# Attention scores on a TensorE-bound kernel: the high-key, low-query term as two products of depth 64 on the two halves of the array's rows

## The chip, the core and the metric

One NeuronCore of one Trainium2 chip runs the whole program. The metric is the time of one execution on the device in microseconds. The kernel before takes 2532.4 us, the median of three runs (2531.88 to 2532.54).

## The reference

Three stages follow each other; everything is float32.

```python
# attention without softmax: u, v [4, 3072, 256], z [4, 3072, 64]
scores = (1 / S) * matmul(z, z.T)
x = u * matmul(maximum(scores, 0) ** 2, v)
# a gated feed-forward (d_ff 1024) on x mixed with the row before it
k = maximum(xk @ w_k, 0);  x = sigmoid(xr @ w_r) * (k * k @ w_v)
# a product of two projections (d_ff 1536)
out = ((x @ w_a) * (x @ w_b)) @ w_out
```

Keys and queries of the scores are the same tensor z, of depth 64; so the matrix of scores is symmetric.

## The kernel before, in words

TensorE multiplies in a rounded form of float32 (`F32R`). To keep the precision of float32, an operand is split into a rounded high part and the rest, the low part, and a product is made of several: high x high, low x high, high x low (`mm3`, L101 to L104).

The attention (`attention`, one call for each of 4 batches x 6 blocks of 512 queries) goes over key blocks of 512 in pairs of 128-key tiles. A pair is one unit of work. Since the scores are symmetric, only blocks with key block >= query block are computed (`scored`); the others are read back from DRAM, where the transposed block was stored (`mirrored`). 42 pairs of a batch are scored, 30 mirrored; over four batches 168 and 120.

A key block lies in `kt` (128 partitions x 512): one half of the partitions holds the 64 dimensions of the high part, the other half those of the low part, and which half is which alternates with the number of the block (`n = s % 2` in `z_prep`). A query block lies in `q` (128 x 2 x 512): `q[:, 0]` is the high part, once in each half of the partitions, `q[:, 1]` the low part, also twice. One matmul of depth 128 with `q[:, 0]` so gives (key high + key low) x query high, one with `q[:, 1]` gives (key high + key low) x query low. For each of the two tiles these two follow each other into one half of a two-bank tile `sc` (L485, L486). ScalarE takes `sc` to `p` (Relu, then Square, L498 and L499), VectorE transposes `p` to store it (L505), ScalarE or VectorE rounds it to `hi` and VectorE makes `lo` (L544 to L547). Then come twelve matmuls of depth 128 into `acc` (two tiles x two halves of v x three).

The order of the work is written out by hand. `units` holds, for each unit, a function that emits the scores and one that emits the twelve value products; the latter follow `AHEAD` = 3 pairs later, so that the scores of a unit stand in front of the value products of an earlier one on TensorE. Work on the side (loads, splits, decoding of weights for later stages) is hung on units by number with `at(i, fn)` and `in_turn(i, ...)`; instructions are emitted in that order, and each engine runs its own in order. Pools of buffers set when a tile may be written again.

z comes in through `z_load` (two blocks of 512 at once, in squares of 32 x 32, by SP's queue), into a tile `zn` of the pool `zp` (one buffer); VectorE transposes the squares from there into `zt` (pool `ztp`, two buffers); `high` and `low` make `kt` of it. The first batch's blocks 2 to 5 come through `zs`.

Of the kernel before, what the change touches and what calls it, by code (L numbers as in the profile page):

```python
# [8 lines left out]
F32 = mybir.dt.float32  # L9
F32R = mybir.dt.float32r  # L10
U32 = mybir.dt.uint32
I32 = mybir.dt.int32
AF = mybir.ActivationFunctionType
ALU = mybir.AluOpType

P = 128
QB = 512
SQ = 32
# [10 lines left out]
def tile_kernel(  # L29
# [29 lines left out]
    nc = tc.nc  # L59
    B, S, D = u.shape  # L60
    DK = z.shape[2]
# [17 lines left out]
    late = {}  # L79
    early = ctx.enter_context(ExitStack())  # L80
    psw = early.enter_context(tc.tile_pool(name="psw", bufs=2, space=bass.MemoryType.PSUM))
    zp = early.enter_context(tc.tile_pool(name="zp", bufs=1))
    ztp = early.enter_context(tc.tile_pool(name="ztp", bufs=2))
    ktp = early.enter_context(tc.tile_pool(name="ktp", bufs=NQB))
    cw = early.enter_context(tc.tile_pool(name="cw", bufs=10))
    turned = early.enter_context(tc.tile_pool(name="turned", bufs=2))
    pmp = early.enter_context(tc.tile_pool(name="pmp", bufs=3))
# [29 lines left out]
    def in_turn(i, *fns):  # L117

        for n, fn in enumerate(fns):
            at(i + n, fn)  # L120
# [236 lines left out]
        at(i, load)  # L357


    zn_t, zt_t, kt_t, v_t, q_t, x_t = {}, {}, {}, {}, {}, {}  # L360

    def z_load(b, s, t=None, queues=()):


        if t is None:
            t = zp.tile([P, QB // SQ, SQ], F32, tag="zn", name="zn")
        for n in range(2):
            src = z[b, (s + n) * QB : (s + n + 1) * QB, :].rearrange("(b i) (a j) -> a i b j", i=SQ, j=SQ)
            for a in range(DK // SQ):
                c = n * DK + a * SQ  # L370
                (queues[a] if queues else nc.sync).dma_start(t[c : c + SQ], src[a])
        zn_t[b, s] = t

    def z_prep(b, s):

        n = s % 2
        h, l = (slice(m * DK, (m + 1) * DK) for m in (n, 1 - n))

        def turn():
            t = zt_t[b, s] = zt_t[b, s + 1] = ztp.tile([P, QB], F32, tag="zt", name="zt")  # L380
            raw = zn_t.pop((b, s)).rearrange("p b j -> p (b j)")
            if b or s:
                nc.vector.transpose(t, raw)
            else:
                nc.vector.transpose(t[:DK], raw[:DK])
                return lambda: nc.vector.transpose(t[DK:], raw[DK:])

        def high():
            kt_t[b, s] = ktp.tile([P, QB], F32R, tag="kt", name="kt")
            if b or s < 2:  # L390
                nc.scalar.activation(kt_t[b, s][h], zt_t[b, s][h], AF.Copy)
            else:
                nc.vector.tensor_copy(kt_t[b, s][h], zt_t[b, s][h])

        def low():
            nc.vector.tensor_tensor(kt_t[b, s][l], zt_t[b, s][h], kt_t[b, s][h].bitcast(F32), op=ALU.subtract)

        return turn, high, low

    def turned_order(t):  # L400

# [6 lines left out]
    def q_prep(b, s):  # L408


        def half(h):
            kt = kt_t[b, s].bitcast(F32)
            if h == 0:
                q_t[b, s] = g_tile([P, 2, QB], F32R, "q")
            q = q_t[b, s]
            m = h ^ s % 2
            k = turned_order(kt[m * DK : (m + 1) * DK])
            nc.vector.tensor_copy(by_order(q[0:DK, h, :]), k)  # L418
            nc.scalar.activation(by_order(q[DK : 2 * DK, h, :]), k, AF.Copy)

        return lambda: half(0), lambda: half(1)
# [48 lines left out]
    def attention(i):  # L470
# [4 lines left out]
        def scored(kb, pr, here):  # L475

            st = {}
            turn = kb > qb

            def a():  # L480
                sc = psw.tile([P, 2, QB], F32, tag="sc", name="sc")
                for t in range(2):
                    c = (2 * pr + t) * P
                    k = kt_t[b, kb][:, c : c + P]
                    nc.tensor.matmul(sc[:, t, :], k, q_t[b, qb][:, 0, :], start=True, stop=False)  # L485
                    nc.tensor.matmul(sc[:, t, :], k, q_t[b, qb][:, 1, :], start=False, stop=True)  # L486
                p = cw.tile([P, 2, QB], F32, tag="cw", name="p")
                if here == 0:
                    hi = cw.tile([P, 2, QB], F32R, tag="cw", name="hi")
                    lo = cw.tile([P, 2, QB], F32R, tag="cw", name="lo")  # L490
                    for t in range(2):
                        nc.scalar.activation(p[:, t, :], sc[:, t, :], AF.Relu, scale=1.0 / S)
                        nc.scalar.activation(p[:, t, :], p[:, t, :], AF.Square)
                        nc.vector.tensor_copy(hi[:, t, :], p[:, t, :])
                        nc.vector.tensor_tensor(lo[:, t, :], p[:, t, :], hi[:, t, :].bitcast(F32), op=ALU.subtract)
                    st["p"] = hi, lo
                    return
                nc.scalar.activation(p, sc, AF.Relu, scale=1.0 / S)  # L498
                nc.scalar.activation(p, p, AF.Square)  # L499
                if turn:  # L500
                    if pr == 0:
                        x_t["turned"] = turned.tile([P, QB // SQ, TPB, SQ], F32, tag="t", name="pt")
                    pt = x_t["turned"]
                    for t in range(2):
                        nc.vector.transpose(  # L505
                            pt[:, :, 2 * pr + t, :], p[:, t, :].rearrange("p (c i) -> p c i", i=SQ)
                        )
                    if pr:
                        d = p_kept[b, kb, qb] = dram.tile(
                            [P, QB // SQ, TPB, SQ], F32, tag=f"p{b}.{kb}.{qb}", name="pkept"  # L510
                        )
                        at(here + 3, lambda: nc.gpsimd.dma_start(d, pt))
                st["p"] = halves(p, turn and (i or pr))


            return st, a
# [97 lines left out]
        if qb == 0:  # L614
            for s in range(0 if b else 1, NQB):
                need = base + s * TPB
                turn, high, low = z_prep(b, s)
                if b:
                    w = base - 16 + (s - NQB + 2) * NKT - 8 * (s < NQB - 1)
                    if s % 2 == 0:  # L620
                        at(w - 6, lambda s=s: z_load(b, s))
                        at(w + 4, turn)
                    in_turn(w + 6, high, low)
                    at(base - 22 + 4 * s, lambda s=s: v_load(b, s))
                    in_turn(base - 16 + 4 * s, *v_prep(b, s))
                    continue
                if s > 1:
                    if s % 2 == 0:
                        at(need - 13, turn)
                    in_turn(max(need - 11, 0), high, low)  # L630
                else:
                    early_z.append((high, low))
                in_turn(need - 1, *v_prep(b, s))
        if i:
            in_turn(base - 7, *q_prep(b, qb))
# [981 lines left out]

    with tc.manual_schedule():
        z_load(0, 0, None, (nc.sync, nc.scalar))
        zs = g_tile([P, 2, QB // SQ, SQ], F32, "zs")  # L1620
        z_load(0, 2, zs[:, 0])
        v_load(0, 0)
        z_load(0, 4, zs[:, 1])
        for n in range(1, NQB):
            v_load(0, n)
        for c, m in enumerate((mu_k, mu_r)):
            nc.sync.dma_start(mu[:, c, :], m.rearrange("(d p) -> p d", p=P))
        turn, high, low = z_prep(0, 0)
        turn_next = turn()
        for fn in (high, low, *q_prep(0, 0), turn_next, *early_z[0]):  # L1630
            fn()
        for n, fn in enumerate(v_prep(0, 0)):
            at(n // 2, fn)
        last = max(len(units), max(sides) + 1)
        for i in range(last):
            if i == n1:
                while pending:
                    pending.popleft()()
                early.close()
                late["ps"] = ctx.enter_context(  # L1640
                    tc.tile_pool(name="psp", bufs=4, space=bass.MemoryType.PSUM, reuse_waits="tile")
                )
                late["p"] = ctx.enter_context(tc.tile_pool(name="late", bufs=24, reuse_waits="tile"))
            for fn in sides.get(i, ()):
                fn()
            if i < len(units):
                a, b, ahead = units[i]
                if a is not None:
                    a()
                if b is not None:  # L1650
                    pending.append(b)
            else:
                ahead = 0
            while len(pending) > ahead:
                pending.popleft()()
# [27 lines left out]
```

## Time and profile before

| | |
|---|---|
| median of three runs | 2532.4 us |
| the profiled execution | 2532.29 us |
| its span, first to last instruction | 2530.5 us |
| TensorE matmul, busy | 2515.5 us, 99% |
| VectorE, busy | 2192.0 us, 87% |
| ScalarE, busy | 1833.7 us, 72% |
| granted TensorE clock | 1.00 of full speed in every slice |

Engines: PE is TensorE's matmul, PEld its loading of weights, DVE VectorE, ACT ScalarE, POOL GpSimd, SP the queue that issues most loads. L485 is line 485 of the kernel. A matmul's record is longer than the distance to the next one, since matmuls are pipelined; the step from start to start is what a matmul costs. The attention takes the span up to about 945 us; the other two stages follow.

### The profile page before, as it was taken

How to read it: one execution, taken by the hardware profiler on the slowest of the kernel's cores; microseconds unless marked ns; L12 is line 12 of the kernel's file. 1: busy time of each engine (PE TensorE's matmuls, PEld its weight loads, DVE VectorE, ACT ScalarE, POOL GpSimd, SP SyncE). 2: the span in 40 equal slices, each digit the busy share in tenths (PEclk: the TensorE clock that was granted, in tenths of full speed). 3: DMA queues.
4: the chain of work that ended last, by engine and by line, in shares of the span. 5: the costliest groups of instructions: out<-in, count | busy, mean ns of one | idle time of the engine just before them, and what ended most of it. 6: DMA issues, size and time to landing. Idle time of an engine off the chain costs nothing.

```text
span 2530.5 us, 32287 instructions
## 1 busy us (share of the span) xinstructions
PE 2515.5 (99%) x11062; PEld 2072.0 (82%) x11062; DVE 2192.0 (87%) x3081; ACT 1833.7 (72%) x2571; POOL 334.9 (13%) x347
## 2 busy tenths in 40 slices
PE   8999999999999999999999999999999999999999
PEld 6888888888888888888888888888888888888887
DVE  9998999899988987888888878888888888888887
ACT  7866977787687758878878766666666766666665
POOL 0110111010000100000000012222222222222211
PEclk9999999999999999999999999999999999999999
DMA  8789789887986894212122156665766675666664
GB/s 216 220 234 239 237 238 232 232 259 219 254 238 200 227 265 155 67 59 92 51 83 67 59 180 219 210 224 184 260 197 231 196 244 196 233 214 220 213 195 138
DMA packets 326629, 486.85 MB, mean 192 GB/s; under 512 B 188800, under 2 KB 202112, under 8 KB 318784
## 3 DMA queue, kind: packets, MB, share of 16 engines
q1 hardware_dynamic: 302880, 372.71, 51.5%
q0 software_dynamic: 21984, 111.42, 11.4%
q8 instruction: 87, 1.43, 0.2%
q10 hardware_dynamic: 1600, 0.66, 0.1%
q14 instruction: 78, 0.64, 0.1%
HBM read 348.13 MB, written 136.58 MB: 192 GB/s over the span
## 4 chain that ended last, share of the span: by engine, by line
PE 98%; DVE 1%; ACT 0%; DMA 0%; issue 0%; DVEq 0%
PE px L1152 15%; PE acc L103 10%; PE acc L104 10%; PE acc L102 10%; PE py L1152 8%; PE vacc L720 6%; PE px L784 5%; PE oacc L1183 4%; PE oacc L1182 4%; PE oacc L1181 4%; PE vacc L744 4%; PE pw L1152 4%; PE sc L486 3%; PE sc L485 3%; PE py L784 3%; PE pw L784 1%
## 5 line engine op out<-in xcount | busy, mean ns | idle before, releaser
L103 PE MATMUL acc<-lo,vhi 128*128 128x512 f32 x1152 | 449.1, 390 | 1.7 <-DVE lo L547 1.4
L102 PE MATMUL acc<-hi,vhi 128*128 128x512 f32 x1152 | 448.4, 389 | 1.1 <-DVE hi L546 1.1
L104 PE MATMUL acc<-hi,vlo 128*128 128x512 f32 x1152 | 448.2, 389 | 0.0
L1152 PE MATMUL px<-t,sw 128*128 128x512 f32 x1296 | 364.3, 389 | 0.0
L1152 PEld LDWEIGHTS px<-t,sw 128*128 128x128 f32 x1296 | 243.0, 188 | 51.2 <-DVE cc L1337 0.6
L103 PEld LDWEIGHTS acc<-lo,vhi 128*128 128x128 f32 x1152 | 216.2, 188 | 49.3 <-DVE lo L547 3.9
L102 PEld LDWEIGHTS acc<-hi,vhi 128*128 128x128 f32 x1152 | 216.2, 188 | 46.8 <-DVE hi L546 1.5
L104 PEld LDWEIGHTS acc<-hi,vlo 128*128 128x128 f32 x1152 | 216.2, 188 | 44.6
L1237 ACT ACTIVATE pw<-px 128x512 f32<-128x512 f32 x144 | 83.8, 582 | 201.3 <-PE px L1152 201.3
L498 ACT ACTIVATE p<-sc 128x1024 f32<-128x1024 f32 x167 | 170.1, 1018 | 69.2 <-PE sc L486 68.1
L1349 POOL TENSOR_TENSOR cc<-cc 128x512 f32<-128x512 f32 x72 | 93.2, 1294 | 873.8 <-DVE b L1203 663.6
L1249 DVE TENSOR_TENSOR u<-py,u 128x512 f32<-128x512 f32 x144 | 99.6, 691 | 124.5 <-PE py L1152 124.5
L547 DVE TENSOR_TENSOR lo<-p,hi 128x1024 fp32r<-128x1024 f32 x167 | 199.9, 1197 | 4.2
L499 ACT ACTIVATE p<-p 128x1024 f32<-128x1024 f32 x167 | 177.3, 1062 | 5.3
L505 DVE STREAM_TRANSPOSE pt<-p 128x512 f32<-128x512 f32 x240 | 155.7, 687 | 25.4 <-ACT p L499 24.9
L1292 ACT ACTIVATE c<-pw 128x512 f32<-128x512 f32 x144 | 86.3, 600 | 110.3 <-PE pw L1152 80.6
L547 DVE TENSOR_TENSOR lo<-pm,hi 128x1024 fp32r<-128x1024 f32 x120 | 145.9, 1217 | 19.7 <-ACT hi L544 19.4
L1347 POOL TENSOR_TENSOR cc<-cc 128x512 f32<-128x512 f32 x71 | 91.7, 1291 | 439.5 <-DVE bl L1203 219.0
L720 PE MATMUL vacc<-kh,w 128*128 128x512 f32 x416 | 143.4, 389 | 0.0
L485 PE MATMUL sc<-q,kt 128*128 128x512 f32 x336 | 132.0, 393 | 6.5 <-DVE q L418 6.4
L544 ACT ACTIVATE hi<-pm 128x1024 fp32r<-128x1024 f32 x120 | 124.8, 1049 | 16.3 <-DMA pm<-pkept 14.2
L486 PE MATMUL sc<-q,kt 128*128 128x512 f32 x336 | 131.7, 392 | 0.0
(251 smaller groups left out, 6111.5 us busy)
## 6 DMA issues: line engine op xcount, KB each, us to landing
sw<-kept SPq DMA_DIRECT2D x252, 512.0 KB, 5.4
pkept<-pt POOLq DMA_DIRECT2D x60, 1024.0 KB, 6.1
pm<-pkept SPq DMA_DIRECT2D x240, 256.0 KB, 6.6
ow<-kept SPq DMA_DIRECT2D x120, 512.0 KB, 6.8
kept<-w POOLq DMA_DIRECT2D x42, 512.0 KB, 5.0
vst<-in_v SPq DMA_DIRECT2D x24, 512.0 KB, 6.8
ust<-in_u SPq DMA_DIRECT2D x192, 64.0 KB, 4.4
xkept<-xr POOLq DMA_DIRECT2D x24, 512.0 KB, 6.4
```

Source lines behind the costliest of these rows:

```text
L102: nc.tensor.matmul(ps, wh, ah, start=first, stop=False)
L103: nc.tensor.matmul(ps, wh, al, start=False, stop=False)
L104: nc.tensor.matmul(ps, wl, ah, start=False, stop=last)
L485: nc.tensor.matmul(sc[:, t, :], k, q_t[b, qb][:, 0, :], start=True, stop=False)
L486: nc.tensor.matmul(sc[:, t, :], k, q_t[b, qb][:, 1, :], start=False, stop=True)
L498: nc.scalar.activation(p, sc, AF.Relu, scale=1.0 / S)
L499: nc.scalar.activation(p, p, AF.Square)
L505: nc.vector.transpose(pt[:, :, 2 * pr + t, :], p[:, t, :].rearrange("p (c i) -> p c i", i=SQ))
L547: nc.vector.tensor_tensor(l, p, h.bitcast(F32), op=ALU.subtract)
L720: nc.tensor.matmul(acc[n, d], x[:, c], y, start=first and m == 0, stop=last and m == 2, skip_group_check=True)
L784: nc.tensor.matmul(bank, w[x][:, c], t[:, y, :], start=first and m == 0, stop=end and m == 2, skip_group_check=True)
L1152: nc.tensor.matmul(bank, w, t[:, y, :], start=first and m == 0, stop=end and m == 2, skip_group_check=True)
```

## The change

A pair's two products with the high query stay as they are. In place of the two products of depth 128 with the low query there are two of depth 64: key high x query low for the first tile on the partitions in which `kt` has the high part, and for the second tile on the other half of the partitions. For that, the high part of every second tile is copied across into a new tile `kx` (`odd`, one ScalarE instruction of 64 x 256 for each block of 512 keys). The term key low x query low is no longer part of the sum. The order of the four becomes high, high, low, low. z is loaded straight into `zt` and transposed in place; the tile `zn` and its pool are gone.

```diff
-    zp = early.enter_context(tc.tile_pool(name="zp", bufs=1))
     ztp = early.enter_context(tc.tile_pool(name="ztp", bufs=2))
     ktp = early.enter_context(tc.tile_pool(name="ktp", bufs=NQB))
+    kxp = early.enter_context(tc.tile_pool(name="kxp", bufs=NQB // 2))
...
     def z_load(b, s, t=None, queues=()):
         if t is None:
-            t = zp.tile([P, QB // SQ, SQ], F32, tag="zn", name="zn")
+            t = ztp.tile([P, QB // SQ, SQ], F32, tag="zt", name="zt")
+            zt_t[b, s] = t.rearrange("p b j -> p (b j)")
...
         def turn():
-            t = zt_t[b, s] = zt_t[b, s + 1] = ztp.tile([P, QB], F32, tag="zt", name="zt")
+            if (b, s) not in zt_t:
+                zt_t[b, s] = ztp.tile([P, QB], F32, tag="zt", name="zt")
+            t = zt_t[b, s + 1] = zt_t[b, s]
...
-        return turn, high, low
+        def odd():
+            if n == 0:
+                kx_t[b, s] = kx_t[b, s + 1] = kxp.tile([P, 2, P], F32R, tag="kx", name="kx")
+            tiles = zt_t[b, s][h].rearrange("p (r t c) -> p r t c", t=2, c=P)[:, :, 1]
+            nc.scalar.activation(kx_t[b, s][l], tiles, AF.Copy)
+
+        return turn, high, low, odd
...
                 sc = psw.tile([P, 2, QB], F32, tag="sc", name="sc")
+                k, q = kt_t[b, kb][:, 2 * pr * P : 2 * (pr + 1) * P], q_t[b, qb]
                 for t in range(2):
-                    c = (2 * pr + t) * P
-                    k = kt_t[b, kb][:, c : c + P]
-                    nc.tensor.matmul(sc[:, t, :], k, q_t[b, qb][:, 0, :], start=True, stop=False)
-                    nc.tensor.matmul(sc[:, t, :], k, q_t[b, qb][:, 1, :], start=False, stop=True)
+                    nc.tensor.matmul(sc[:, t, :], k[:, t * P : (t + 1) * P], q[:, 0, :], start=True, stop=False)
+                h, l = (slice(m * DK, (m + 1) * DK) for m in (kb % 2, 1 - kb % 2))
+                nc.tensor.matmul(sc[:, 0, :], k[h, :P], q[h, 1, :], start=False, stop=True)
+                nc.tensor.matmul(sc[:, 1, :], kx_t[b, kb][l, pr, :], q[l, 1, :], start=False, stop=True)
...
-                turn, high, low = z_prep(b, s)
+                turn, *rounded = z_prep(b, s)
...
-        turn, high, low = z_prep(0, 0)
+        turn, high, low, odd = z_prep(0, 0)
         turn_next = turn()
-        for fn in (high, low, *q_prep(0, 0), turn_next, *early_z[0]):
+        for fn in (high, low, *q_prep(0, 0), odd, turn_next, *early_z[0]):
```

On TensorE, in the middle of the first batch, a scored pair before stands like this between value products (`sc`, the scores; `kt`, the key; numbers are those of buffers):

```order
L104 MATMUL acc_2341<-hi_2307,vlo_2097 128x512
L485 MATMUL sc_2421<-q_2158,kt_1675 128x512
L486 MATMUL sc_2421<-q_2158,kt_1675 128x512
L485 MATMUL sc_2421<-q_2158,kt_1675 128x512
L486 MATMUL sc_2421<-q_2158,kt_1675 128x512
L102 MATMUL acc_2340<-hi_2336,vhi_2096 128x512
```

At the like place in the changed kernel (`kx` is the copy across):

```order
L104 MATMUL acc_2354<-hi_2381,vlo_2152 128x512
L493 MATMUL sc_2497<-q_2171,kt_2025 128x512 x2
L495 MATMUL sc_2497<-q_2171,kt_2025 128x512
L496 MATMUL sc_2497<-q_2171,kx_2056 128x512
L102 MATMUL acc_2353<-hi_2413,vhi_2151 128x512
```

The two products with the high query now stand together, and the two of depth 64 stand behind them; the number of matmuls is the same.

On ScalarE, at the start of the program, before (L391 is the key's high part, L419 the query's lower half of partitions, L492 and L493 the first scores by halves, L498 the second unit's):

```order
L391 ACTIVATE kt<-zt 64x512
L419 ACTIVATE q<-kt 64x512 x2
L391 ACTIVATE kt<-zt 64x512
L492 ACTIVATE p<-sc 128x512
L493 ACTIVATE p<-p 128x512
L492 ACTIVATE p<-sc 128x512
L493 ACTIVATE p<-p 128x512
L498 ACTIVATE p<-sc 128x1024
```

And in the changed kernel:

```order
L394 ACTIVATE kt<-zt 64x512
L428 ACTIVATE q<-kt 64x512 x2
L405 ACTIVATE kx<-zt 64x256
L394 ACTIVATE kt<-zt 64x512
L405 ACTIVATE kx<-zt 64x256
L502 ACTIVATE p<-sc 128x512
L503 ACTIVATE p<-p 128x512
L502 ACTIVATE p<-sc 128x512
L503 ACTIVATE p<-p 128x512
L405 ACTIVATE kx<-zt 64x256
L508 ACTIVATE p<-sc 128x1024
```

Three copies across (L405) stand among the first instructions: behind the query, behind the second key, and before the second unit's scores. Further 21 stand behind the later keys.

## Rows read from the trace of the kernel before

**Rows 1.** The page's busy times by engine, over the whole span.
```profile
PE 2515.5 (99%) x11062; PEld 2072.0 (82%) x11062; DVE 2192.0 (87%) x3081; ACT 1833.7 (72%) x2571; POOL 334.9 (13%) x347
```
**Rows 2.** The page's chain that ended last, by engine.
```profile
PE 98%; DVE 1%; ACT 0%; DMA 0%; issue 0%; DVEq 0%
```
**Rows 3.** Waits, 20 to 945 us: us in total, times, longest us.
```profile
ACT hi L544 <- DMA pm<-pkept: 14.2, 3, 7.5
...
PE acc L103 <- DVE lo L547: 0.6, 2, 0.3
```
**Rows 4.** TensorE around one scored pair in order of time: start us, us, what.
```profile
303.85 0.39 PE L485 MATMUL sc<-q,kt 128*128 128x512 f32 x1
303.85 0.19 PEld L486 LDWEIGHTS sc<-q,kt 128*128 128x128 f32 x1
304.08 0.39 PE L486 MATMUL sc<-q,kt 128*128 128x512 f32 x1
...
304.53 0.39 PE L486 MATMUL sc<-q,kt 128*128 128x512 f32 x1
...
304.76 0.39 PE L102 MATMUL acc<-hi,vhi 128*128 128x512 f32 x1
```
**Rows 5.** Busy time by stage, 20 to 920 us: us, engines (x instructions), PEclk, DMA.
```profile
20.00:920.00 900.00, 899.27 (x3963) 742.94 (x3962) 835.14 (x1243) 689.13 (x776) 91.59 (x150) 1.00 0.84 233
```
**Rows 6.** Groups by line, the score matmuls: busy us, mean ns | idle before.
```profile
L485 PE MATMUL sc<-q,kt 128*128 128x512 f32 x336 | 132.0, 393 | 6.5 <-DVE q L418 6.4
L486 PE MATMUL sc<-q,kt 128*128 128x512 f32 x336 | 131.7, 392 | 0.0
```
**Rows 7.** Order of time near the end: a weight load that was waited for.
```profile
2515.39 0.19 PEld L1183 LDWEIGHTS oacc<-l,ow 128*128 128x128 f32 x1 [0.43 <-DVE l L1203]
2515.39 0.50 PE L1183 MATMUL oacc<-l,ow 128*128 128x512 f32 x1
...
2515.73 0.39 PE L1181 MATMUL oacc<-h,ow 128*128 128x512 f32 x1
```
**Rows 8.** Order of time at the end: sixteen transposes of 128 columns on TensorE.
```profile
2522.80 1.83 PEld L1504 LDWEIGHTS pt<-one,ot 128*128 128x128 f32 x16 [0.43 <-issue]
2522.83 2.04 PE L1504 MATMUL pt<-one,ot 128*128 128x128 f32 x16
```
**Rows 9.** Busy time in slices of 20 us: six of 46, the first and the last among them.
```profile
20.00:40.00 20.00, 19.27 (x83) 15.00 (x82) 19.64 (x30) 15.82 (x19) 1.24 (x2) 1.00 0.71 190
...
60.00:80.00 20.00, 20.00 (x90) 16.57 (x89) 19.97 (x31) 17.45 (x19) 1.06 (x2) 1.00 0.30 110
...
300.00:320.00 20.00, 20.00 (x90) 16.57 (x89) 19.95 (x33) 16.56 (x19) 3.57 (x6) 1.00 0.63 220
320.00:340.00 20.00, 20.00 (x90) 16.57 (x89) 15.98 (x21) 16.96 (x19) 1.23 (x2) 1.00 1.05 265
...
480.00:500.00 20.00, 20.00 (x90) 16.57 (x89) 19.30 (x29) 19.36 (x22) 1.09 (x2) 1.00 0.72 180
...
920.00:940.00 20.00, 20.00 (x90) 16.57 (x89) 16.20 (x24) 8.14 (x9) 0.69 (x1) 1.00 1.00 200
```
**Rows 10.** The same slices, instructions on the tile sc alone: first, third, last.
```profile
20.00:40.00 20.00, 6.25 (x24) 4.51 (x24) 0.00 (x0) 5.10 (x5) 1.00 0.71 190
...
60.00:80.00 20.00, 5.34 (x20) 3.75 (x20) 0.00 (x0) 5.11 (x5) 1.00 0.30 110
...
920.00:940.00 20.00, 0.00 (x0) 0.00 (x0) 0.00 (x0) 0.00 (x0) 1.00 1.00 200
```
**Rows 11.** Groups by line, ScalarE, two small shapes.
```profile
L391 ACT ACTIVATE kt<-zt 64x512 fp32r<-64x512 f32 x20 | 12.6, 628 | 7.2 <-DVE zt L383 4.5 <-DVE zt L385 1.4 <-DVE zt L386 1.0
...
L281 ACT ACTIVATE w<-val 128x256 fp32r<-128x256 f32 x9 | 3.6, 402 | 0.0
```
**Rows 12.** ScalarE at the start in order of time.
```profile
5.82 0.63 ACT L419 ACTIVATE q<-kt 64x512 fp32r<-64x512 f32 x1
...
7.46 0.63 ACT L391 ACTIVATE kt<-zt 64x512 fp32r<-64x512 f32 x1 [1.02 <-DVE zt L386]
...
8.49 0.60 ACT L492 ACTIVATE p<-sc 128x512 f32<-128x512 f32 x1 [0.40 <-PE sc L486]
```

More of the change, by code (lines that the diff above doesn't have):

```diff
@@ L357, in weight @@
         at(i, load)
-    zn_t, zt_t, kt_t, v_t, q_t, x_t = {}, {}, {}, {}, {}, {}
+    zn_t, zt_t, kt_t, kx_t, v_t, q_t, x_t = {}, {}, {}, {}, {}, {}, {}
     def z_load(b, s, t=None, queues=()):
         if t is None:
-            t = zp.tile([P, QB // SQ, SQ], F32, tag="zn", name="zn")
+            t = ztp.tile([P, QB // SQ, SQ], F32, tag="zt", name="zt")
+            zt_t[b, s] = t.rearrange("p b j -> p (b j)")
         for n in range(2):
@@ L622, in attention @@
                         at(w + 4, turn)
-                    in_turn(w + 6, high, low)
+                    in_turn(w + 6, *rounded)
                     at(base - 22 + 4 * s, lambda s=s: v_load(b, s))
@@ L629, in attention @@
                         at(need - 13, turn)
-                    in_turn(max(need - 11, 0), high, low)
+                    in_turn(max(need - 11, 0), *rounded)
                 else:
-                    early_z.append((high, low))
+                    early_z.append(rounded)
                 in_turn(need - 1, *v_prep(b, s))
```

## The prediction

> **What bounds the kernel now.** I read the page's busy shares first, then the chain, then who waited for whom, then the instructions around the scores in order of time. TensorE is busy 2515.5 of 2530.5 us, VectorE 2192.0, ScalarE 1833.7 [rows 1]. The chain that ended last is TensorE for 98% of the span [rows 2]. Over the attention after its start (20 to 945 us) TensorE waited 0.6 us in all, for a low part from VectorE [rows 3]. So whatever TensorE issues, the kernel pays in full, and what another engine does costs nothing until TensorE has to wait for it.
>
> The price of one TensorE step comes from the steady rows: in a score pair the matmuls of L485, L486, L485, L486 and the next L102 begin 0.91 us apart over four steps, 0.227 us each, though one record lasts 0.39 us [rows 4]. The stretch from 20 to 920 us says the same: 899.27 us over 3963 matmuls is 0.227 [rows 5]. Records overlap by 389 - 227 = 162 ns: that is the tail of a product that lies under the next one. Each weight load starts as the matmul before it starts, and is hidden.
>
> **The change part by part.** *The scores.* There are 336 + 336 score matmuls, four to a pair of key tiles, so 168 pairs [rows 6]. After the change a pair still issues four matmuls with four weight loads: two of depth 128 (both halves of the key against the high query), then two of depth 64, one on array rows 0 to 63 and one on 64 to 127, into the two halves of `sc`. Their number does not fall, so a gain can only come from the last two running at the same time. No matmul of this trace has a depth under 128, so this must be bounded.
>
> Upper bound: they overlap wholly, and a pair costs three steps in place of four: 168 x 0.227 = 38.1 us saved. For that, both small weight loads must be done while the second deep product runs. The tail's sixteen 128-column loads take 1.83 us, (1.83 - 0.19) / 15 = 0.109 us apart [rows 8], so two take 0.22 us and just fit into a step of 0.227. [...]
>
> Lower bound: the switch from depth 128 to 64 and back empties the array. Then each switch shows the tail that lies hidden now, 162 ns, and a pair costs 2 x 162 - 227 = 97 ns more than before: 16.3 us lost. If the weights of the new kind cannot be loaded ahead either, each switch also shows a load. What a load costs when it is not hidden stands at 2515.39 us: the matmul that waited for its weights lasts 0.50 us in place of 0.39, 0.11 us more [rows 7]. Then a pair costs 2 x (162 + 110) - 227 = 317 ns more, 53 us in all.
>
> Between ends so far apart I take the upper one as the start of the sum, because the nearest row is the steady one [rows 4]: there a weight load already proceeds under a running product of other weights, and a load of 64 rows in the idle half asks for no more.
>
> *What then becomes late.* VectorE and ScalarE make the same `p`, `hi`, `lo` and `pt` from scores that come faster. I cut 20 to 940 us into 46 slices of 20 us. In each I compared the saving (score matmuls in the slice / 4 x 0.227) [rows 10] with VectorE's idle time [rows 9]. From 20 to 40 us six pairs would save 1.36, but VectorE has 0.36 free; from 60 to 80, five pairs 1.13 against 0.03. From 300 to 320 it has 0.05 free, from 320 to 340 it has 4.02, more than any slice would save. The smaller of the two, summed over the 46 slices, is 25.2 us. TensorE runs three pairs behind the scores, about 3 x 16 x 0.227 = 11 us, so part of a shortage is bridged, but less than a slice. I take 28 of the 38.1 us: near 25.2, a little above.
>
> *The copy across.* 24 new ScalarE copies of 64x256 (one per 512 keys). The nearest rows: 128x256 takes 0.40 us, 64x512 takes 0.63 [rows 11]; so 0.40 each, 9.7 us on an engine that has 900 - 689 = 211 us free [rows 5]. They lie beside TensorE's steady stream; where ScalarE is full (19.36 of 20 us from 480 to 500 [rows 9]) one costs at most its 0.40 us, and three or four such places 1 to 2 us, within the range. The new wait is that of L496 for this copy. Behind it on TensorE stand the unit's twelve value products; but after the first two blocks the copy is emitted at least 4 units, two pairs or 7 us, ahead of its use, so I charge no wait.
>
> *The start.* There TensorE waits for the others, so copies count. The first stands behind the query's two halves: ScalarE ends these at 6.45 and is idle until 7.46 [rows 12], so it is hidden. The second stands behind the next key (ends 8.09) and before the first `p`, which waits until 8.49 for the score: hidden by 0.40, just. The third stands before the second unit's `p`, where ScalarE has no gap: 0.4 to 0.5 us late. I charge 0.5.
>
> *z in place.* The transposes keep their number, place and shape on VectorE; SP's loads keep their places in the queue. A load now waits for the readers of the tile two loads back, of the batch before or earlier: long done. Cost: nothing. The shortest cover is that of the second batch's first load, some 14 units after the last reader of its tile, 7 x 16 x 0.227 = 25 us; if it were gone, TensorE would wait for the next batch's keys, once.
>
> **Sum.** The profiled execution took 2532.29 us (span 2530.5 and 1.8 around it), 0.1 below the median of 2532.4. 2532.3 - 28 + 0.5 = 2504.8; beside the median 2505.
>
> **Rivals.** *One product after the other in part.* If the second small weight load starts only when the first small product starts, as each load in the steady rows does [rows 4], the second product starts 110 to 188 ns after the first. A pair saves 117 to 39 ns: 20 to 7 us, 2513 to 2526. For it: every load in the rows stands exactly so. [...] The DMA ends here as well: its share is 1.05 from 320 to 340 us [rows 9], and a load of mirrored scores held up ScalarE three times, 14.2 us in all [rows 3]; if it binds in those of the 46 slices that have a share of 1.00 or more (13), 9 of the 28 us are lost.
>
> *Slower: the array empties at every switch.* 336 switches, two for each pair, in the steady stream. From 2532.3 + 16 = 2549 (tails alone) to 2585 (tails and loads). It decides from 113 ns a switch on, half a step; below that the change still gains. For it: 162 ns of tail are there to be shown, and the pairs stand singly between runs of twelve deep products, so nothing shares a switch. Against: nothing in the trace switches, so nothing shows that a product must wait for the tail of another. [...]
>
> *It does not do what it says.* The two small products run one after the other at 0.227 us each and a switch costs nothing: four steps as before, 2532, with at most 1 us for the copies.
>
> **How the numbers follow.** Full overlap 0.44 (2494 to 2508, its own range: 38.1 us saved down to 25), partial overlap 0.14, no overlap, or a switch that just eats the gain, 0.09, emptying 0.33. This measurement can tell 0.2% from no change, about 5 us. Faster 0.58, same 0.09, slower 0.33. The range begins at 2493, just below the upper bound, and goes to 2572: beyond it lies the worse part of the emptying case, about 0.12.
>
> **What would show it.** Right: the L496 matmuls start a few ns after L495, the next L102 0.227 us later; a pair and its twelve deep products take 15 steps, 3.40 us where neither VectorE nor ScalarE is waited for, not 3.63; TensorE shows waits for `lo` and `hi` between 20 and 100, 260 and 320, and 480 and 560 us that were not there. VectorE's busy time is as before, ScalarE's 9.7 us more. Emptying right: a gap of 0.16 to 0.27 us before L495 and before the L102 behind it, and no waits for VectorE. Partial right: L496 starts 0.11 to 0.19 us after L495. The stages after the attention are unchanged in length; should they differ, the sum above is wrong in a place I did not look at.

## The result, and the profile after

The changed kernel takes 2563.4 us (median of four runs, 2563.25 to 2563.62), the one before 2532.4 in the same comparison: a ratio of 1.0123, 95% interval 1.0105 to 1.0140. It is slower by 31.0 us; the forecast was 27 us faster. The profiled execution has a span of 2561.6 us, 31.1 more than before.

The page's busy times, which answer to [rows 1], and its chain, which answers to [rows 2]:

```profile
PE 2547.8 (99%) x11062; PEld 2028.9 (79%) x11062; DVE 2193.6 (86%) x3081; ACT 1848.0 (72%) x2595; POOL 334.6 (13%) x347
...
PE 99%; SPq 0%; DMA 0%; DVE 0%; issue 0%; DVEq 0%
```

TensorE still sets the end, with as many matmuls as before, 32 us longer busy. VectorE's work is the same; ScalarE's is 14 us more, 10 of it the copies across. To see where the 31 us are, two cuts of the busy time by stage, first of the kernel before, then of the changed one (length, then each engine's busy time and instructions, granted clock, DMA share, GB/s):

```profile
20.00:950.00 930.00, 929.27 (x4095) 767.79 (x4094) 855.19 (x1270) 700.56 (x788) 92.95 (x152) 1.00 0.84 235
950.00:2531.00 1581.00, 1574.82 (x6934) 1296.46 (x6932) 1322.30 (x1789) 1118.34 (x1764) 241.75 (x191) 1.00 0.51 167
```

```profile
20.00:981.00 961.00, 960.89 (x4095) 724.72 (x4095) 856.74 (x1269) 714.21 (x810) 92.70 (x152) 1.00 0.81 227
...
981.00:2562.00 1581.00, 1574.87 (x6936) 1297.26 (x6934) 1322.88 (x1790) 1118.49 (x1764) 241.71 (x191) 1.00 0.50 167
```

The same 4095 matmuls take 930 us before and 961 after; everything behind the attention takes 1581 in both. So the whole loss lies in the attention. Who TensorE waited for after its first product, in the changed kernel, against [rows 3] (total, times, longest, in us):

```profile
PE acc L103 <- DVE lo L557: 0.8, 1, 0.8
PE acc L102 <- DVE hi L556: 0.2, 1, 0.2
```

Both of these waits lie before 20 us. From there to the end TensorE waits for no other engine. One pair in order of time, against [rows 4] (start, length of the record, what):

```profile
306.12 0.41 PEld L493 LDWEIGHTS sc<-q,kt 128*128 128x128 f32 x2
306.34 0.61 PE L493 MATMUL sc<-q,kt 128*128 128x512 f32 x2
...
306.89 0.18 PEld L495 LDWEIGHTS sc<-q,kt 64*128 64x128 f32 x1 [0.35 <-issue]
306.89 0.50 PE L495 MATMUL sc<-q,kt 64*128 64x512 f32 x1
306.89 0.18 PEld L496 LDWEIGHTS sc<-q,kx 64*128 64x128 f32 x1
306.89 0.50 PE L496 MATMUL sc<-q,kx 64*128 64x512 f32 x1
307.32 0.19 PEld L102 LDWEIGHTS acc<-hi,vhi 128*128 128x128 f32 x1 [0.24 <-issue]
307.32 0.50 PE L102 MATMUL acc<-hi,vhi 128*128 128x512 f32 x1
...
307.43 0.19 PEld L103 LDWEIGHTS acc<-lo,vhi 128*128 128x128 f32 x1
307.66 0.40 PE L103 MATMUL acc<-lo,vhi 128*128 128x512 f32 x1
...
308.81 0.39 PE L102 MATMUL acc<-hi,vhi 128*128 128x512 f32 x1
```

Three things are to be seen. The two small products start at the same time, 306.89: they overlap wholly. The second deep product starts one step into the two-matmul row, at about 306.57; the small ones follow 0.32 us later, not 0.227, and the value product follows them by 0.43 (0.32 and the 0.11 of the next sentence). And the weight loads of both changes start no earlier than their own matmul, whose record is 0.50 us long in place of 0.39: 0.11 us of load is in the open, as where a matmul waited for its weights in [rows 7]. From the first deep product to the L103 behind the pair it is 307.66 - 306.34 = 1.32 us; before, five steps of 0.227, 1.135. The difference of 0.185 us, 168 times, is 31 us.

So one change of depth costs 0.32 + 0.11 - 0.227 = 0.20 us: 0.09 until the next product starts, and 0.11 for a load that does not go ahead. Reckoned back from the 31 us, with the step saved, it is (0.185 + 0.227) / 2 = 0.206.

That one pair gives just 31 us is in part luck: it is a little longer than most, and a smaller third part of the cost lies behind it. Over the 162 single pairs after 20 us, the median time from the first score product to the second value product is 1.306 us, before 1.133; and the ten steps behind that take 2.287 us, before 2.267. The first difference is 0.173, the second 0.020: 0.193 a pair, some 32 us in 168 pairs, against the 31.6 by which TensorE is busy longer in the two cuts above. The 0.206, reckoned from the whole loss, holds all three parts.

### The profile page after: what moved, and what is told of

Read it like the earlier page. It is cut to its first block, busy times and chain, and to the rows that moved or that the text cites. A ratio compares the mean times of both kernels' runs of the same rounds, so it can differ in the third digit from the quotient of the medians.

```text
span 2561.6 us, 32312 instructions
## 1 busy us (share of the span) xinstructions
PE 2547.8 (99%) x11062; PEld 2028.9 (79%) x11062; DVE 2193.6 (86%) x3081; ACT 1848.0 (72%) x2595; POOL 334.6 (13%) x347
## 4 chain that ended last, share of the span: by engine, by line
PE 99%; SPq 0%; DMA 0%; DVE 0%; issue 0%; DVEq 0%
PE px L1162 15%; PE acc L102 11%; PE acc L103 10%; PE acc L104 10%; PE py L1162 8%; PE vacc L730 6%; PE px L794 5%; PE oacc L1193 4%; PE oacc L1192 4%; PE oacc L1191 4%; PE vacc L754 4%; PE pw L1162 4%; PE sc L493 3%; PE sc L495 3%; PE py L794 3%; PE pw L794 1%
## 5 line engine op out<-in xcount | busy, mean ns | idle before, releaser
L102 PE MATMUL acc<-hi,vhi 128*128 128x512 f32 x1152 | 467.6, 406 | 0.2 <-DVE hi L556 0.2
L103 PE MATMUL acc<-lo,vhi 128*128 128x512 f32 x1152 | 450.6, 391 | 0.9 <-DVE lo L557 0.8
L104 PE MATMUL acc<-hi,vlo 128*128 128x512 f32 x1152 | 448.9, 390 | 0.0
L102 PEld LDWEIGHTS acc<-hi,vhi 128*128 128x128 f32 x1152 | 216.2, 188 | 80.8 <-issue 35.1
L104 PEld LDWEIGHTS acc<-hi,vlo 128*128 128x128 f32 x1152 | 216.5, 188 | 46.6
L103 PEld LDWEIGHTS acc<-lo,vhi 128*128 128x128 f32 x1152 | 216.7, 188 | 41.0 <-DVE lo L557 1.7
L554 ACT ACTIVATE hi<-p 128x1024 fp32r<-128x1024 f32 x115 | 122.1, 1061 | 3.7
L794 PE MATMUL px<-t,w 128*128 128x512 f32 x432 | 121.6, 390 | 0.0
```

The source lines that it names most:

```text
L102: nc.tensor.matmul(ps, wh, ah, start=first, stop=False)
L103: nc.tensor.matmul(ps, wh, al, start=False, stop=False)
L104: nc.tensor.matmul(ps, wl, ah, start=False, stop=last)
L554: nc.scalar.activation(h, p, AF.Copy)
L794: nc.tensor.matmul(bank, w[x][:, c], t[:, y, :], start=first and m == 0, stop=end and m == 2, skip_group_check=True)
```

## The experiments

The theory was that price for each change between depth 128 and depth 64, in either direction, and a whole overlap of the two small products. The rivals were the work beside it, a wait of the small product for the bank that a deep one had just left, and an overlap that is only in the records.

**No small products, all else kept.**

```diff
-                nc.tensor.matmul(sc[:, 0, :], k[h, :P], q[h, 1, :], start=False, stop=True)
-                nc.tensor.matmul(sc[:, 1, :], kx_t[b, kb][l, pr, :], q[l, 1, :], start=False, stop=True)
+                for t in range(2):
+                    nc.tensor.matmul(sc[:, t, :], k[:, t * P : (t + 1) * P], q[:, 1, :], start=False, stop=True)
```

> Keeps the copy across, z in place and the order high, high, low, low, but makes both low products of depth 128 again (so key low x query low is in the sum again, and the copy is not used). Theory (each switch between depths costs 0.205 us: 0.09 until the array is empty, 0.11 for a weight load that cannot go ahead; the two small products overlap wholly): no switch, four steps of 0.227 us a pair, so 2532 us, within 2. Rival (the side work costs: copies on ScalarE, the order of the four): it stays well above 2532, up to 2563.

Measured: 2532.5 us against 2532.3, ratio 1.000 (0.9991 to 1.001). The copies across, z in place and the order of the four cost nothing. The busy row of this kernel shows the cover: ScalarE has 10.6 us more than in [rows 1] and TensorE 0.5.

```profile
PE 2516.0 (99%) x11062; PEld 2074.8 (82%) x11062; DVE 2191.9 (87%) x3081; ACT 1844.3 (73%) x2595; POOL 334.8 (13%) x347
```

**Small products first.** The two small products, with `start=True`, ahead of the two deep ones.

> The two products of depth 64 come first in the pair, the two of depth 128 behind them. Theory of the switch: still two switches a pair, 2563 us, within 2; the gap before the small ones stays at 0.09 us + 0.11 for the load. Rival (a small product waits because it adds into a bank that a deep product has only just left): as the first into its bank it does not wait, 0.09 x 168 = 16 us less, 2548.

Measured: 2563.7 us. The order of time of this kernel shows the small products behind a value product, into a bank that was free:

```profile
306.30 0.39 PE L104 MATMUL acc<-hi,vlo 128*128 128x512 f32 x1
306.62 0.50 PE L493 MATMUL sc<-q,kt 64*128 64x512 f32 x1
306.62 0.50 PE L494 MATMUL sc<-q,kx 64*128 64x512 f32 x1
307.05 0.73 PE L496 MATMUL sc<-q,kt 128*128 128x512 f32 x2
```

They come 0.32 us after L104, just as they came after the deep score product. So it is not a bank just left by a deep product that holds them up, and the rival's 2548 is out.

**One small product left out.**

```diff
-                nc.tensor.matmul(sc[:, 1, :], kx_t[b, kb][l, pr, :], q[l, 1, :], start=False, stop=True)
```

> Leaves out the second small product (key high x query low of the second tile). Theory: it lies wholly beside the first one, so its removal saves nothing: 2563 us, within 2. Rival (the overlap is only in the records, and the two run one after the other in the array): 0.227 x 168 = 38 us less, 2525.

Measured: 2564.9 us, nothing saved. The second product of a pair is free beside the first. It is even 1.5 us more, and the trace shows where: the ten steps behind the second value product take 2.302 us in the mean in place of 2.290, which is 2.1 us over 168 pairs. Why they are longer stays open.

**Four changes of depth in a pair.** The order high, low, high, low.

```diff
+                nc.tensor.matmul(sc[:, 0, :], k[:, :P], q[:, 0, :], start=True, stop=False)
+                nc.tensor.matmul(sc[:, 0, :], k[h, :P], q[h, 1, :], start=False, stop=True)
+                nc.tensor.matmul(sc[:, 1, :], k[:, P:], q[:, 0, :], start=True, stop=False)
+                nc.tensor.matmul(sc[:, 1, :], kx_t[b, kb][l, pr, :], q[l, 1, :], start=False, stop=True)
```

> The order is high, low, high, low, so a pair has four switches and its small products no neighbour to overlap with. Theory: 4 x 0.205 = 0.82 us a pair over the four steps of before, 138 us in all, 2670 us, within 8. Rival (the cost belongs to a small product that adds to a deep one, two of them in a pair, not to each change of depth): 2 x 0.205 x 168 = 69 us, 2601.

Measured: 2670.8 us, 138.4 more than before; 138.4 / (4 x 168) = 0.206 us a change. One pair of it:

```profile
308.43 0.39 PE L493 MATMUL sc<-q,kt 128*128 128x512 f32 x1
308.75 0.18 PEld L494 LDWEIGHTS sc<-q,kt 64*128 64x128 f32 x1 [0.35 <-issue]
308.75 0.50 PE L494 MATMUL sc<-q,kt 64*128 64x512 f32 x1
...
309.18 0.49 PE L495 MATMUL sc<-q,kt 128*128 128x512 f32 x1
...
309.60 0.49 PE L496 MATMUL sc<-q,kx 64*128 64x512 f32 x1
...
310.02 0.50 PE L102 MATMUL acc<-hi,vhi 128*128 128x512 f32 x1
```

Behind every change stands a record of 0.50 and a step of 0.42 to 0.43, whichever way it goes. This and the changed kernel give the same price from different sums, and the rival's 2601 is out.

**Both small products on one half of the rows.** The second reads `k[h, P:]` and `q[h, 1, :]`.

> Both small products use the same half of the array's rows (that in which kt has the high part), so they cannot overlap; the two switches of a pair stay. Theory (switch 0.206 us from the measured 31.0 us: (31.0/168 + 0.227)/2; overlap of two products on different halves is whole): one step of 0.227 us more for each pair than in the changed kernel, 2563.4 + 38.1 = 2601.5 us, within 2. Rival (a product on the rows that the one before it uses also waits for it, or for its weights): 0.09 to 0.2 us more a pair, 2617 to 2636.

Measured: 2606.2 us, 42.8 over the changed kernel: outside the theory's 2 us, and short of the rival's 2617. The overlap is bound to the two halves of the rows, and is worth the step that the theory gave it, 38 us. Most of the 4.7 us over that lies in the steps behind the return: the ten behind the second value product take 2.309 us in the mean in place of 2.290, 3.3 us over 168 pairs; here it is 0.24 us from L103 to L104. Why is open:

```profile
310.69 0.29 PEld L496 LDWEIGHTS sc<-q,kt 64*128 64x128 f32 x2 [0.35 <-issue]
310.69 0.73 PE L496 MATMUL sc<-q,kt 64*128 64x512 f32 x2
...
311.35 0.50 PE L102 MATMUL acc<-hi,vhi 128*128 128x512 f32 x1
...
311.69 0.40 PE L103 MATMUL acc<-lo,vhi 128*128 128x512 f32 x1
...
311.93 0.40 PE L104 MATMUL acc<-hi,vlo 128*128 128x512 f32 x1
```

The rows show one thing more. The second small load ends at 310.98, the end of its two-load row, and its product starts at 311.02 (two records in 0.73 us, the second 0.39 long): this load did go ahead, under a product on the same rows. So what did not go ahead is not the load of a small product as such, but the load across a change of depth.

**Half as many changes.** Both pairs of a key block are scored at once: four deep products, then two overlapping steps of small ones.

```diff
+                group = (pr,) if here == 0 or (i == 0 and kb == 0) else (0, 1)
+                if pr == group[0]:
...
+                    for r in group:
+                        nc.tensor.matmul(sc_t[r][:, 0, :], k(r, 0)[h], q[h, 1, :], start=False, stop=True)
+                        nc.tensor.matmul(sc_t[r][:, 1, :], kx_t[b, kb][l, r, :], q[l, 1, :], start=False, stop=True)
```

> The scores of both pairs of a key block are emitted together: four deep products, then four of depth 64 in two overlapping steps (the program's first key block stays as it is). 83 groups, so half the switches. Theory: a group costs 2 x 0.206 + 6 x 0.227 in place of 8 x 0.227 of before, 0.042 us less; 83 x 0.042 = 3.5 us less, and 0.4 more for the two pairs at the start: 2529 us if nothing else waits. Rival (both score tiles are taken at once, so TensorE waits for ScalarE to empty them, or value products wait for a later p): more than 2532, by what the same grouping without small products shows.

The control has the same grouping with eight deep products:

> The grouping of two pairs alone: eight deep products together, no product of depth 64 (key low x query low is in the sum; the copy across is made and not used). Theory: no switches and as many steps as before, 2532 us where the score tiles come free in time. Rival (TensorE waits for the score tiles): more than 2532, and the two-pair kernel with small products lies about 3 us below this one, whatever this one takes.

Measured: 2541.5 us with small products (ratio 1.0039, 1.0025 to 1.0053), 2535.0 without (1.0011). So 22 of the 31 us are back, as fewer changes should do, but 2529 was not reached. Up to the return a group does what the theory says; in order of time the second step of small products comes 0.34 after the first, a step and the open load:

```profile
310.03 1.07 PE L499 MATMUL sc<-q,kt 128*128 128x512 f32 x4
311.02 0.49 PE L502 MATMUL sc<-q,kt 64*128 64x512 f32 x1
...
311.36 0.39 PE L502 MATMUL sc<-q,kt 64*128 64x512 f32 x1
...
311.69 0.50 PE L102 MATMUL acc<-hi,vhi 128*128 128x512 f32 x1
```

From 310.03 to where L102's stream starts (311.69 + 0.11) it is 1.77 us, against eight steps of 0.227, 1.816. Most of what was lost are waits for ScalarE, which has to empty both score tiles (whom TensorE waited for, total, times, longest):

```profile
PE sc L499 <- ACT p L516: 6.7, 7, 2.7
```

Behind the longest of these a second price shows (three stretches of time, the column after the engines is the granted clock):

```profile
566.00:568.00 2.00, 1.78 (x7) 1.05 (x8) 2.00 (x5) 1.94 (x3) 0.76 (x2) 0.91 1.02 411
568.00:570.40 2.40, 2.40 (x7) 1.85 (x6) 1.72 (x3) 2.37 (x4) 1.01 (x2) 0.50 1.04 409
570.40:576.00 5.60, 5.60 (x25) 4.59 (x24) 4.59 (x5) 3.62 (x4) 0.00 (x0) 0.94 1.09 350
```

Behind 2.68 us without a product the clock was granted at 0.50 of full speed, for some seven products. It fell only after the products had begun again at 566.22: the stretch from 566 to 568 still has 0.91.

**The waits taken out.** ScalarE takes both pairs out of the score tiles at once; the first two key blocks of the program are single pairs with deep products.

```diff
+                        for r in group:
+                            p_t[r] = cw.tile([P, 2, QB], F32, tag="cw", name="p")
+                            nc.scalar.activation(p_t[r], sc_t[r], AF.Relu, scale=1.0 / S)
```

> As the two-pair kernel with small products, but ScalarE takes both pairs out of the score tiles at once (Relu of both, then the rest of each in its turn), and the program's first two key blocks for the first queries are single pairs with deep products (their key low x query low is in the sum). Theory (what the two-pair kernel lost were TensorE's waits for ScalarE at the score tiles, about 10 us): these go, and 82 groups save 0.042 us each: 3.5 us below the same kernel with deep products, 2529 if that one takes 2532. Rival (the waits come from elsewhere, or a small product in a group costs more than its step): 2535 or more.

> The same order and the same early Relu, but all products deep (key low x query low is in the sum; the copy across is made and not used). Theory: no switches and no waits at the score tiles, so 2532 to 2533. Rival (early Relu pushes the rest of ScalarE's work back, and TensorE waits for value operands): 2534 or more.

Measured: 2534.0 us with small products, 2534.2 without; both 1.0008 of before (0.9999 to 1.0017). The waits at the score tiles are gone (0.5 us are left with small products, none without), and with them 7.6 of the 12.5 us that lay between the two-pair kernel's 2541.5 and its 2529. But the 3.5 us between the two kernels did not come: 0.2. Both now wait for VectorE a little more, as the control's rival said (first with small products, then without):

```profile
PE acc L103 <- DVE lo L576: 3.7, 5, 1.3
PE acc L102 <- DVE hi L575: 1.1, 1, 1.1
PE sc L500 <- ACT p L512: 0.5, 2, 0.3
```

```profile
PE acc L103 <- DVE lo L568: 2.6, 4, 0.9
PE acc L102 <- DVE hi L567: 1.1, 1, 1.1
```

That is a difference of 1.6 us, but the profiled execution of the first took 2535.5, 1.6 above its median, so it may not be the usual one. The larger part is in the steps behind each return. One group of either kernel, first with small products, then without:

```profile
301.44 1.07 PE L500 MATMUL sc<-q,kt 128*128 128x512 f32 x4
...
303.44 0.39 PE L103 MATMUL acc<-lo,vhi 128*128 128x512 f32 x1
...
305.73 0.39 PE L104 MATMUL acc<-hi,vlo 128*128 128x512 f32 x1
```

```profile
300.82 0.39 PE L499 MATMUL sc<-q,kt 128*128 128x512 f32 x1
...
302.86 0.39 PE L103 MATMUL acc<-lo,vhi 128*128 128x512 f32 x1
...
305.12 0.39 PE L104 MATMUL acc<-hi,vlo 128*128 128x512 f32 x1
```

To the second value product it is 2.00 us against 2.04, and the ten steps behind that take 2.29 against 2.26. The medians of all 82 groups are 2.002 against 2.040 and 2.292 against 2.267. So a group saves 0.038 - 0.025 = 0.013 us and not 0.042: 1.1 us in all, not 3.5. Why 0.2 us is left of that 1.1, whether by the waits for VectorE or by chance, stays open. Of all forms tried, none is faster than the kernel before.

## Why the prediction was wrong

- **What bounds the kernel:** right. TensorE pays for each of its steps, and the loss of 31 us is found on it whole, and behind the first 20 us it waits for no other engine.
- **The upper bound, whole overlap:** right as a mechanism. The two products start within 0.01 us of each other, and leaving one out saves nothing (2564.9 us against 2563.4). That L496 would start "a few ns" after L495 stands in no row of the kernel before; in the changed kernel's trace it is 3 ns, the median of the 162 single pairs after 20 us.
- **The step that failed** is the choice between the ends: "I take the upper one as the start of the sum, because the nearest row is the steady one", a load under a running product of other weights. That row shows a load of the same depth as the product above it, and the "idle half" of the sentence is not idle while a product of depth 128 runs (128*128 in its record). The runs show that it does not hold across a change of depth: there the load starts with its own matmul, and the matmul itself not before 0.32 us after the last. The rival of a cost at every change, priced at 97 to 317 ns a pair and given 0.33, is what happens; its measured price is 185 ns.
- **The sizes in that rival:** the open load was right, 0.11 us [rows 7]. The tail was too large: of the 162 ns that lie hidden, 93 come to light. With 93 in place of 162, 2 x (93 + 110) - 227 = 179 ns a pair, 30 us. The rival's turning point, 113 ns a change, was worked out rightly: 206 is nearly twice that. What the runs show is that every change cost time, 0.206 us. That the array is empty in between, as the rival and the first experiment's theory have it, was the author's assumption; the rows do not show it, as 69 of the 162 ns stay hidden.
- **VectorE as the next bound** (28 of 38 us kept): not reached, as TensorE became slower. Its waits for `lo` and `hi` are 1.0 us in the changed kernel, so neither these 28 us nor the DMA's part in them was put to the test. The price of the DMA rival was also misread: its 9 us are what the 13 slices hold of the whole 38.1; of the 25.2 that VectorE would leave they hold 7.3.
- **The copies, z in place, the start:** right. 24 copies take 0.416 us each, and the control with deep products is at 2532.5.
- **The range** ended at 2572 and held 2563.4; the direction, at 0.58 for faster, was wrong.

## What to carry to other kernels

Two products on the two halves of the array's rows did run in the time of one here (both start at 306.89), but going from full depth to half depth and back cost 0.206 us each way in an otherwise dense stream, nearly a step of 512 columns (0.227). Saved steps must be counted against changes: here one step was saved for two changes, and with two steps for two changes it was a draw. A row in which a cost is hidden speaks only for the same kind of neighbour; where the change makes a new kind, the hidden parts (a record's tail, a weight load) are the first candidates for what will show.

## What the runs showed of the hardware that was not expected

- Of the 162 ns by which a matmul record outlasts its step, 93 ns show at a change of depth; the rest stays hidden. Why it is not all of it is open. That the 110 ns are the load is read from the rows alone, and no run changed the one part without the other; a small product with fewer weight columns might, and was not tried.
- The steps behind a return to full depth are a little longer than 0.227 us, up to 0.24: 0.020 us over ten steps in the changed kernel, 0.025 behind a group. That was enough to take most of what a group saves.
- Once, a wait of 2.68 us in the middle of dense work was followed by a granted clock of 0.50 for more than 2 us, which cost at least 1.2 us beyond the wait itself (in order of time, six steps of 0.427 us between the starts at 568.08 and 570.64, in place of 0.227). It is one case; that the wait brought the clock down was not shown.
